# Sixteen block products for h, a tangent for the decay, and turned keys read in place

## The chip, the cores and the metric

The kernel runs on one core of a Trainium2 chip. The metric is the device time of one execution, in microseconds (us). A core has TensorE (PE in the profile; PEld are its weight loads), VectorE (DVE), ScalarE (ACT), GpSimd (POOL) and SyncE (SP), which issues the transfers. The engines run side by side and meet through semaphores; each takes its own instructions in a fixed order.

## The reference

A recurrent attention feeds a two-layer network. Per batch (4) and head (8), over 768 tokens, with head size 48:

```
f = 1 / (1 + exp(-f_logit))
for t in range(S):
    state = f[:, :, t, :, None] * state + outer(k[:, :, t], v[:, :, t])
    y[:, :, t] = q[:, :, t] @ state
x = y as (3072 tokens, 384)
h = x @ w_in                      # 384 x 2048
g = h * (1 / (1 + exp(-1.702 * h)))
out = g @ w_out                   # 2048 x 384
```

Everything is float32 on the chip. The weights come in as 64-bit floats and are turned into 32-bit ones on the way in.

## The kernel before

The 3072 tokens are 12 units of 256 tokens, three to a batch. `attention(n)` makes a list of parts for unit n: levels of scores (kinds V, V3, W), the turned keys (C, C2 or T), the state update (S), and the loading and turning of the next unit's decay, queries and keys (B, B2, K3). Each level multiplies queries by keys on PE (L392, tile `sc`), scales queries and keys by products of the decay on DVE (`promote`, L473 and L477), sets copies of them aside on ACT (L448 `Kc`, L454 `Qc`), and moves the scores under a mask into `A` (L421, L441). The products of the decay are `tot`, made by POOL in `begin_gates` (L383). At the end of a unit, y is copied from PSUM (L627, `yT`) and moved by transfers to `xT`, where the 384 features lie on the partitions (`to_x`).

The network's work is the fill between these parts. `merge(n, fill, ...)` emits the parts of unit n and, after each, as many matmul columns of the fill as the part's share says. For units 0 to 2 the network is done in blocks of four feature tiles (`mlp_blocks`), because the weights are still arriving and being converted by `convert` (L217 to L222). From unit 3 on, `mlp_unit(n)` does a whole unit: `mlp_h` (16 feature tiles of 128, three matmuls of 256 columns each, L785, with a gelu on ACT, L789), then `mlp_o7`, which makes the four blocks of the output with seven block products instead of eight (L762); its sums of g are made on DVE by `sums_of_a` and `last_sum` (L698 to L707), and its sums of w_out once by `sums_of_b`.

What sets the order: up to the merge of unit 3 every engine keeps the program's order; after that only PE does, and a scheduler orders the other engines. On PE, each network product waits in line; nothing overtakes it.

What the change touches:

- `turn` and `begin_f`: the decay is turned to features on partitions, by PE and ACT for units 0 to 2 (L344, L349), by DVE for later ones (L332), and goes through the sigmoid into `F` (L337 for later units, L355 for unit 2). Gelu and sigmoid are in different activation tables, so that ACT loads a table (an instruction ACT_TABLE_LOAD) at each change.
- `fetch_k`: keys of units 4 to 10 are turned by way of DRAM; two copies per unit (L555) put them in `kn` in the order in which the state update (L576) reads them.
- PSUM: four banks under one tag `mm`, taken in turn by whatever product comes next.
- `vr`, the values to be reversed, in two buffers; `g`, six quarter buffers.

Of the kernel before, what the change touches and what calls it, by code (L numbers as in the profile page):

```python
# [23 lines left out]
def kernel(  # L24
# [37 lines left out]
    P = 128  # L62
# [37 lines left out]
    A = const.tile([P, 2 * NP, 2, HS], F32, name="A")  # L100

    def keep_up(times, columns=384, of=None):

        if times:
            pt = ps.tile([P, columns], F32, tag="mm", name=f"idle_{next(serial)}", bufs=4)
        for _ in range(times):
            lhs, rhs = of or (ident, masks.rearrange("p l f t -> p (l f t)"))
            nc.tensor.matmul(pt, lhsT=lhs, rhs=rhs, start=True, stop=True)  # L108
# [117 lines left out]
    def convert():  # L226

        if state["begin"] < len(pairs) and len(todo) <= NOP // 2:
            begin_pair(state["begin"])
            state["begin"] += 1  # L230
        if todo and todo[0]:
            todo.pop(0)()
        if todo and todo[0] is None:
            todo.pop(0)
            state["done"] += 2
            fetch_weights()

# [40 lines left out]
    def load_v(n):  # L278


        if n >= NALL:
            return
        b, s0 = n // NU, n % NU * U
        vts[n] = ld.tile([P, 2, DM], F32, tag="vt", name=f"vt_{n}", bufs=2)
        vrs[n] = ld.tile([P, DM], F32, tag="vr", name=f"vr_{n}", bufs=2)
        nc.sync.dma_start(
            out=vts[n][:, 1].rearrange("p (h d) -> p h d", h=H), in_=v[b, :, s0:s0 + HALF, :].rearrange("h p d -> p h d")
        )
        for i in range(4):
            t0 = s0 + U - 32 * (i + 1)  # L290
            nc.sync.dma_start(
                out=vrs[n][32 * i:32 * (i + 1)].rearrange("p (h d) -> p h d", h=H),
                in_=v[b, :, t0:t0 + 32, :].rearrange("h p d -> p h d"),
            )
# [11 lines left out]
    def attention(n):  # L306
# [19 lines left out]
        def turn(j, outs, fn=None):  # L326

            if n >= N_FILL:
                for f in (1, 0):
                    out = outs(f)  # L330
                    at, step = (0, 1) if f else (HALF - 1, -1)
                    nc.vector.transpose(  # L332
                        view(out, at, [[HALF, NP], [step, R4], [R4 * step, 32]]),
                        by_half[:, j, f].rearrange("p a (j d) -> p (a j) d", j=R4)[:, :, :32],
                    )
                if fn:
                    nc.scalar.activation(F, F, fn)  # L337
                return
            for j0 in range(0, R, 4):
                pt = ps.tile([P, 4, P], F32, tag="mm", name=f"t_{n}_{j}_{j0}", bufs=4)  # L340
# [6 lines left out]
                for f in (1, 0):  # L347
# [4 lines left out]
                        fn if fn and n < N_FILL - 1 else AF.Copy,  # L352
                    )
            if fn and n == N_FILL - 1:
                nc.scalar.activation(F, F, fn)  # L355

        def begin_f():
            turn(0, lambda f: F[:, ORDER.index(f) * SLOT:(ORDER.index(f) + 1) * SLOT], AF.Sigmoid)
            if n >= N_FILL or (n == 1 and 0 == 0):
                load_raw(n + 1, 0)  # L360
# [164 lines left out]
        def turn_k(a0):  # L525
            if a0 == 0:
                new_kn()
            pt = ps.tile([P, 2, 2, P], F32, tag="mm", name=f"tkn_{n}_{a0}", bufs=4)
# [21 lines left out]
        def fetch_k(f):  # L550
            if f == 0:
                new_kn()
            z = mlp.tile([P, P, NP], F32, tag="sum", name=f"kt_{n}_{f}", bufs=3)
            nc.sync.dma_start(out=z.rearrange("p d a -> p (d a)"), in_=k_toks[n % 2][f].rearrange("t i x -> t (i x)"))
            nc.scalar.copy(t["kn"][:, :, f, :], z.rearrange("p d a -> p a d"))  # L555
# [12 lines left out]
        def _():  # L568
            add()
            pd = scores().rearrange("p h a s t -> p h (a s t)")  # L570
            for a in range(NP):
                for f in (1, 0):
                    for h in range(2):
                        for g in range(NG):
# [3 lines left out]
                                lhsT=t["kn"][g * HS:(g + 1) * HS, a, f, h * HS:(h + 1) * HS],  # L578
# [20 lines left out]
        def _():  # L599
# [21 lines left out]
            xT = xTs[n] = mlp.tile([P, NK, width(n)], F32, tag="xT", name=f"xT_{n}", bufs=3)  # L621
            for f in (1, 0):
# [6 lines left out]
            if n == NALL - 1:  # L629

                pl = ps.tile([P, NP], F32, tag="mm", name="y_last", bufs=4)
# [10 lines left out]
                to_x(lambda h: (yl[rows(h), :NK], lambda r, d: yl[r:r + d, NK]), xT[:, :, U:], 1)  # L642
# [48 lines left out]
    def sums_of_a(n, g, b):  # L691

        j = b % 2
        t0, t1 = slice(0, G), slice(G, 2 * G)
        tt = nc.vector.tensor_tensor
        if b < 2:
            g["S", j] = mlp.tile([P, FG, width(n)], F32, tag="g", name=f"S_{n}_{j}", bufs=6)
            tt(g["S", j][:, :, t1], g[j][:, :, t0], g[j][:, :, t1], ALU.subtract)  # L698
        else:
            tt(g[j][:, :, t1], g[j][:, :, t1], g[j + 2][:, :, t1], ALU.add)  # L700
            tt(g["S", j][:, :, t0], g[j][:, :, t1], g[j][:, :, t0], ALU.subtract)

    def last_sum(n, g):

        for j in range(2):
            by = slice(0, G)
            nc.vector.tensor_tensor(g[j + 2][:, :, by], g[j + 2][:, :, by], g["S", j][:, :, by], ALU.subtract)  # L707

    def mlp_o7(n, g):
        a = lambda i, j: lambda f: g[j * 2 + f // FG][:, f % FG, i * G:(i + 1) * G]  # L710
        s = lambda i: lambda f: g["S", f // FG][:, f % FG, i * G:(i + 1) * G]
        b = lambda i, j: lambda f: quarter(w_out, i, j)[:, f]
        T_ = lambda i: lambda f: T[i][:, f] if i < 4 else T[4](f)
        t = {}

        def out_(tt):
            if "o" not in g:
                g["o"] = mlp.tile([P, U // P, DM], F32, tag="osb", name=f"osb_{n}", bufs=1)
            return g["o"][:, tt]

        def row(name):
            t[name] = mlp.tile([P, HC], F32, tag=name, name=f"{name}_{n}", bufs=1)
            return t[name]

        def p1():
            nc.scalar.copy(row("p1"), t["X"])

        def p4():
            nc.scalar.copy(row("p4"), t["W"])

        def p2():
            nc.scalar.copy(out_(0)[:, :HC], t["X"])
            last_sum(n, g)

        def p6():
            nc.scalar.copy(row("p6"), t["Y"])

        def p5():
            nc.scalar.copy(row("p5"), t["Z"])

        def p7():
            nc.vector.tensor_tensor(row("u3"), t["p1"], t["Y"], ALU.add)
            nc.vector.tensor_tensor(out_(1)[:, :HC], t["u3"], t["p4"], ALU.subtract)
            nc.vector.tensor_tensor(out_(1)[:, HC:], t["u3"], t["p5"], ALU.add)
            store(n, 1, out_(1))

        def p3():
            nc.vector.tensor_tensor(out_(0)[:, HC:], t["p1"], t["Z"], ALU.add)
            nc.vector.tensor_tensor(out_(0)[:, HC:], out_(0)[:, HC:], t["p6"], ALU.add)
            store(n, 0, out_(0))  # L750


        products = (
            ("X", a(0, 0), b(0, 0), p1, True), ("W", a(1, 1), T_(4), p4, True), ("X", a(0, 1), b(1, 0), p2, False),
            ("Y", s(0), T_(2), p6, True), ("Z", a(1, 0), T_(1), p5, True), ("Y", s(1), T_(3), p7, False),
            ("Z", a(0, 1), b(1, 1), p3, False),
        )

        def one(bank, lhs, rhs, done, new, f):
            if new and f == 0:  # L760
                t[bank] = ps.tile([P, HC], F32, tag="mm", name=f"o_{n}_{bank}", bufs=4)
            nc.tensor.matmul(  # L762
                t[bank], lhsT=lhs(f), rhs=rhs(f), start=(new and f == 0), stop=(f == HF - 1), skip_group_check=True,
            )
            if f == HF - 1:
                done()
        return [(HC, lambda p=p, f=f: one(*p, f), 0) for p in products for f in range(HF)]


    xTs = {}  # L770

    def width(n):

        return U + (n == NALL - 1)

    def mlp_h(n, ffs, g, sums=False):
        t = {}

        def one(ff, c):
            if c == 0:  # L780
                if ff % FG == 0:
                    g[ff // FG] = mlp.tile([P, FG, width(n)], F32, tag="g", name=f"g_{n}_{ff}", bufs=6)
                t["ph"] = ps.tile([P, width(n)], F32, tag="mm", name=f"h_{n}_{ff}", bufs=4)
# [4 lines left out]
            if c == NK - 1:  # L788
                nc.scalar.activation(g[ff // FG][:, ff % FG, :], ph, AF.Gelu_apprx_sigmoid)  # L789
                if sums and ff % FG == FG - 1:  # L790
                    sums_of_a(n, g, ff // FG)
                if width(n) > U:

                    by = g[ff // FG][:, ff % FG, U:]
                    if ff == 0:
                        g["last"] = mlp.tile([P, 1, DM], F32, tag="sum", name="sum_last", bufs=3)
                        nc.vector.tensor_scalar(g["last"][:, 0], w_out[:, 0, :], by, None, op0=ALU.mult)
                    else:
                        nc.vector.scalar_tensor_tensor(
                            g["last"][:, 0], w_out[:, ff, :], by, g["last"][:, 0], op0=ALU.mult, op1=ALU.add  # L800
                        )
        return [(NK * U, lambda ff=ff: [one(ff, c) for c in range(NK)], ff // FG * NPC + ff % FG + 1) for ff in ffs]

    def mlp_o(n, ffs, g, done):
# [3 lines left out]
        def one(tt, ff):  # L808
            if ff == ffs[0]:
                t["po"] = ps.tile([P, DM], F32, tag="mm", name=f"o_{n}_{tt}_{ff}", bufs=4)  # L810
# [13 lines left out]
    def mlp_unit(n):  # L824
        g = {}

        def last_token():
            po = ps.tile([P, DM], F32, tag="mm", name="o_last", bufs=4)
# [4 lines left out]
        if width(n) > U:  # L833
            o.insert(3 * HF, (DM, last_token, 0))
        return mlp_h(n, range(NFF), g, True) + o
# [19 lines left out]
    def mlp_blocks(*blocks):  # L855

        hs, os = zip(*(mlp_block(n, r) for n, r in blocks))
        return sum(hs, []) + sum(os, [])
# [92 lines left out]
    UNIT = NFF * NK * U + U // P * NFF * DM  # L951

# [21 lines left out]
    fill += mlp_blocks((2, 0), (2, 1)) + mlp_blocks((2, 2), (0, 3)) + mlp_blocks((1, 3), (2, 3))  # L974
# [7 lines left out]
    for n in range(4, NALL):  # L982
        merge(n, fill, NFF * NK * U + 7 * HF * HC, late, chores=list(sums_of_b()) if n == 4 else ())
# [31 lines left out]
```

## Time and profile before

| | us |
|---|---|
| median of three runs | 628.49 |
| lowest, highest | 628.22, 629.21 |
| span of the profiled execution | 627.9 |
| PE, PEld busy | 602.8, 517.5 |
| DVE, ACT, POOL busy | 385.8, 260.3, 39.9 |
| h matmuls of all units (L785), busy | 257.4, of which 20.85 in the last unit |
| output matmuls of units 3 to 11 (L762), busy | 179.2 |

The profile is one execution. Busy time is the time in which an engine has at least one instruction running. A float32 matmul is two MATMUL records and two LDWEIGHTS records. "Idle before" names what an engine waited for last. The page's first parts give each engine's share, and then its busy tenths in forty slices of the span; the chain of work that ended last is followed back from the end, and its shares say which engine set the time.

### The profile page before, as it was taken

The numbers are of one execution on the slowest core, as the hardware profiler recorded it, in microseconds if no ns is written. First come the engines' busy times: TensorE is split into PE (matmuls) and PEld (weight loads), VectorE is DVE, ScalarE is ACT, GpSimd is POOL, SyncE is SP. The second block draws the span as 40 slices with busy tenths as digits, with TensorE's granted clock in tenths as the row PEclk, the third lists the DMA queues.
The fourth block names the chain that finished last, engine by engine and source line by source line (L and its number), as shares of the span: only waits on it lengthen the run. The fifth ranks groups of instructions, "written<-read, shape, count | busy, mean of one in ns | idle before, by whom it ended". The sixth has DMA issues, their size and how long they took to land.

```text
span 627.9 us, 17094 instructions
## 1 busy us (share of the span) xinstructions
PE 602.8 (96%) x7314; PEld 517.5 (82%) x7314; DVE 385.8 (61%) x632; ACT 260.3 (41%) x544; POOL 39.9 (6%) x91
## 2 busy tenths in 40 slices
PE   7958999889999999999999999999999999999997
PEld 5647776757678688989989989989989889889896
DVE  1778976575876755677566577656658645521441
ACT  3436543533244534543544454354354353233220
POOL 3010030020001001001001001001001001000000
PEclk9898999989999999999999999999999999999999
DMA  7646675652034444444452342552161121001000
GB/s 171 183 126 165 170 161 158 148 139 76 2 92 99 122 100 105 105 94 110 122 135 60 76 109 73 142 123 68 45 160 33 44 59 27 27 1 27 26 1 25
DMA packets 83308, 58.20 MB, mean 93 GB/s; under 512 B 33633, under 2 KB 75265, under 8 KB 83233
## 3 DMA queue, kind: packets, MB, share of 16 engines
q1 hardware_dynamic: 82192, 55.55, 35.4%
q10 hardware_dynamic: 1041, 1.57, 1.0%
q8 instruction: 57, 0.93, 0.7%
q14 instruction: 18, 0.15, 0.1%
HBM read 43.98 MB, written 8.39 MB: 83 GB/s over the span
## 4 chain that ended last, share of the span: by engine, by line
PE 87%; DVE 6%; ACT 3%; DMA 2%; issue 1%; SPq 1%; ACTq 0%; DVEq 0%
PE h L785 38%; PE o_X L762 8%; PE o_Y L762 8%; PE o L811 8%; PE o_Z L762 7%; PE sc L392 6%; PE o_W L762 4%; PE t L344 3%; PE y L616 2%; PE sc L576 2%; PE y L488 1%; PE idle L108 1%; DVE a L221 1%; DMA xT<-yT 1%; ACT yT L627 1%
## 5 line engine op out<-in xcount | busy, mean ns | idle before, releaser
L785 PE MATMUL h<-xT,w_in 128*128 128x256 f32 (+1 forms) x1152 | 257.4, 381 | 2.4 <-ACT g L789 1.9
L785 PEld LDWEIGHTS h<-xT,w_in 128*128 128x128 f32 x1152 | 216.4, 190 | 34.2 <-ACT g L789 2.1
L789 ACT ACTIVATE g<-h 128x256 f32<-128x256 f32 (+1 forms) x192 | 72.0, 383 | 156.8 <-PE h L785 156.5
L477 DVE TENSOR_TENSOR X<-X,tot 128x1024 f32<-128x1024 f32 x45 | 55.1, 1224 | 62.6 <-PE sc L392 49.4
L448 ACT COPY Kc<-X 128x512 f32<-128x512 f32 x72 | 48.0, 666 | 83.4 <-DVE X L477 51.3
L811 PE MATMUL o<-w_out,g 128*128 128x384 f32 x192 | 67.5, 501 | 3.0 <-DVE w_out L222 3.0
L811 PEld LDWEIGHTS o<-w_out,g 128*128 128x128 f32 x192 | 36.2, 194 | 26.0 <-DVE w_out L222 3.6
L762 PE MATMUL o_X<-w_out,g 128*128 128x192 f32 x288 | 52.6, 331 | 0.0
L762 PE MATMUL o_Y<-T,S 128*128 128x192 f32 x288 | 51.9, 329 | 0.0
L441 DVE COPY_PREDICATED A<-masks,sc 128x256 f32<-128x256 uint32 (+1 forms) x108 | 50.9, 534 | 0.1
L762 PEld LDWEIGHTS o_Y<-T,S 128*128 128x128 f32 x288 | 46.9, 190 | 1.5 <-issue 0.7
L762 PEld LDWEIGHTS o_X<-w_out,g 128*128 128x128 f32 x288 | 46.7, 190 | 1.0
L383 POOL TENSOR_TENSOR tot<-F 128x512 f32<-128x512 f32 x12 | 12.5, 1039 | 478.2 <-DVE st L594 429.3
L392 PE MATMUL sc<-X,Kc 48*64 48x64 f32 x1440 | 31.1, 224 | 10.7 <-ACT Kc L448 9.6
L392 PEld LDWEIGHTS sc<-X,Kc 48*64 48x64 f32 x1440 | 26.4, 138 | 18.0 <-ACT Kc L448 11.4
L332 DVE STREAM_TRANSPOSE X<-raw 128x512 f32<-128x512 f32 x36 | 37.9, 1101 | 2.9 <-PE y L616 2.8
L700 DVE TENSOR_TENSOR g<-g,g 128x512 f32<-128x512 f32 x18 | 12.5, 692 | 40.4 <-ACT g L789 40.4
L627 ACT COPY yT<-y 48x256 f32<-48x256 f32 x92 | 33.7, 366 | 7.8 <-PE y L616 5.3
L473 DVE TENSOR_TENSOR X<-X,tot 128x512 f32<-128x512 f32 x30 | 20.3, 688 | 13.1 <-PE sc L392 11.0
L383 POOL TENSOR_TENSOR tot<-tot 128x256 f32<-128x256 f32 (+4 forms) x60 | 24.6, 410 | 4.7
L762 PE MATMUL o_W<-T,g 128*128 128x192 f32 x144 | 24.9, 326 | 0.0
L762 PE MATMUL o_Z<-w_out,g 128*128 128x192 f32 x144 | 24.9, 326 | 0.0
(92 smaller groups left out, 629.1 us busy)
## 6 DMA issues: line engine op xcount, KB each, us to landing
bits<-in_moe_w_out_dram SPq DMA_DIRECT2D x8, 768.0 KB, 5.0
raw<-in_f_logit_dram SPq DMA_DIRECT2D x48, 96.0 KB, 2.3
raw<-in_k_dram SPq DMA_DIRECT2D x48, 96.0 KB, 2.3
raw<-in_q_dram SPq DMA_DIRECT2D x44, 96.0 KB, 2.3
bits<-in_moe_w_in_dram SPq DMA_DIRECT2D x7, 576.0 KB, 6.2
k_tok<-z SPq DMA_DIRECT2D x56, 64.0 KB, 1.8
kt<-k_tok SPq DMA_DIRECT2D x14, 256.0 KB, 2.8
out_dram<-osb SPq DMA_DIRECT2D x18, 192.0 KB, 1.8
```

The lines of the kernel that those rows point to most:

```text
L332: nc.vector.transpose(view(out, at, [[HALF, NP], [step, R4], [R4 * step, 32]]), by_half[:, j, f].rearrange("p a (j d) -> p (a j) d", j=R4) ...
L383: nc.gpsimd.tensor_tensor(tn, t2[:, :, 0], t2[:, :, 1], ALU.mult)
L392: nc.tensor.matmul(t["sc"][g * HS:(g + 1) * HS, h, a, s, :], lhsT=t["Kc", l][rows(h), x:x + HS], rhs=rhs(h, a, g), start=True, stop=True,)
L441: nc.vector.copy_predicated(out=view(A, at, dims), mask=mask.bitcast(U32), data=got)
L448: nc.scalar.copy(c.rearrange("p (n two m) -> p n two m", two=2, m=m), view(X, KF * SLOT, [[2 * m, SLOT // (2 * m)], [(KR - KF) * SLOT + m, ...
L473: nc.vector.tensor_tensor(x, x, y, ALU.mult)
L477: nc.vector.tensor_tensor(x, x, y, ALU.mult)
L627: copy(view(yT[rows(h)], at, [[U, NP], [step, HS]]), py[columns(h, g), g, :, f, :])
L762: nc.tensor.matmul(t[bank], lhsT=lhs(f), rhs=rhs(f), start=(new and f == 0), stop=(f == HF - 1), skip_group_check=True,)
L785: nc.tensor.matmul(ph, lhsT=w_in[:, c, ff * P:(ff + 1) * P], rhs=xTs[n][:, c, :], start=(c == 0), stop=(c == NK - 1))
L789: nc.scalar.activation(g[ff // FG][:, ff % FG, :], ph, AF.Gelu_apprx_sigmoid)
L811: nc.tensor.matmul(t["po"], lhsT=g[ff // FG][:, ff % FG, tt * P:(tt + 1) * P], rhs=w_out[:, ff, :], start=(ff == ffs[0]), stop=(ff == ffs[ ...
```

## The change

1. **h by sixteen products.** For units 3 to 11, w_in (15 of its 16 feature tiles) is seen as 3 by 3 blocks: three groups of five feature tiles by three groups of 128 input features. x of a unit is 3 by 2 blocks: three groups of features by two halves of 128 tokens. The plain product of such blocks takes 18 block products; a bilinear scheme does it in 16, of sums of blocks. `mlp_h16` runs them in four lanes, each with a PSUM bank of its own. A lane is a chain of products that add up in the bank; on the way the running sum is read out after some products (by an ACT copy the first time a block of h is met, by a DVE add the second time), so that one bank serves several blocks. The sixteenth feature tile is done as before (`left`).
2. **Sums of w, once.** `sums_of_w` makes the blocks' sums in unit 3 (seven new tiles N1 to N7) and some in place of blocks of w_in that earlier units no longer need (`middle`, `last`), 14 operations on POOL and 4 on DVE.
3. **Sums of x, per unit.** `sums_of_x` makes eleven operations of 128x128 on POOL once xT is there.
4. **Decay by the tangent.** sigmoid(x) = 0.5 tanh(x/2) + 0.5. ACT makes the tanh, POOL the 0.5 and 0.5. Where the kernel before has twenty table loads, the built kernel has two.
5. **Turned keys read with a step.** The copies to `kn` go; the state update reads the weights from the fetched tile with a step of four elements.
6. **Room.** PSUM banks are named (`mm0` to `mm3`, function `bank`), a few products move to the scores' buffer `sc`, `vr` has one buffer, `g` three half buffers. `mlp_o7` keeps its sums in the output tile instead of rows of its own, and takes the feature tiles in the order in which h gets ready. `sums_of_a` runs after all of h instead of between its quarters.

```diff
-                    nc.scalar.activation(F, F, fn)
+                    fn()
...
+        def half_up():
+            nc.gpsimd.tensor_scalar(F, F, 0.5, 0.5, op0=ALU.mult, op1=ALU.add)
+
+        def sigmoid():
+            nc.scalar.activation(F, F, AF.Tanh, scale=0.5)
+            half_up()
...
         def fetch_k(f):
-            if f == 0:
-                new_kn()
-            z = mlp.tile([P, P, NP], F32, tag="sum", name=f"kt_{n}_{f}", bufs=3)
+            z = t["kt", f] = mlp.tile([P, P, NP], F32, tag="sum", name=f"kt_{n}_{f}", bufs=3)
             nc.sync.dma_start(out=z.rearrange("p d a -> p (d a)"), in_=k_toks[n % 2][f].rearrange("t i x -> t (i x)"))
-            nc.scalar.copy(t["kn"][:, :, f, :], z.rearrange("p d a -> p a d"))
+        def turned_k(p, a, f, d):
+            return t["kt", f][p, d, a] if n in CARRY else t["kn"][p, a, f, d]
...
+    CHAINS = (
+        (("D5", "b21", 3), ("N6", "E12", 2), ("C4", "E4", 4), ("N3", "E15", 0), ("a00", "E6", 1), ("N4", "E10", 5)),
+        (("N5", "b21", None), ("N1", "b11", 1), ("D11", "E11", None), ("D8", "E3", 0)),
+        (("a22", "E3", None), ("D9", "E9", 4), ("N7", "b10", None), ("N2", "E14", 2)),
+        (("a10", "E0", None), ("D2", "b11", 3)),
+    )
+    LANES = ((0, 0), (1, 3)), ((0, 1), (1, 1)), ((0, 2), (1, 2)), ((0, 3), (1, 0))
...
+            for t in range(nt):
+                x = (ts.start + t) * P
+                nc.tensor.matmul(
+                    ph[:, t], lhsT=WA[a][:, x:x + P], rhs=E[n][b], start=(i == 0 and t == 0),
+                    stop=(i == len(CHAINS[chain]) - 1), skip_group_check=True,
+                )
+            if out is None:
+                return
+            to = where(group, out // 2, out % 2)
+            scale = -1.0 if out in NEGATIVE else 1.0
+            if out == CHAINS[0][-1][2]:
+                nc.scalar.activation(to, ph, AF.Gelu_apprx_sigmoid, scale=scale)
+            elif (group, out) not in begun:
+                begun.add((group, out))
+                nc.scalar.copy(to, ph)
+            else:
+                nc.vector.tensor_tensor(to, to, ph, ALU.add)
+                nc.scalar.activation(to, to, AF.Gelu_apprx_sigmoid, scale=scale)
...
-        return mlp_h(n, range(NFF), g, True) + o
+        return mlp_h16(n, g) + o
...
-        merge(n, fill, NFF * NK * U + 7 * HF * HC, late, chores=list(sums_of_b()) if n == 4 else ())
+        merge(n, fill, H16 + 7 * HF * HC, late, chores=list(sums_of_b()) if n == 4 else ())
```

A chain's entry is the block or sum of w, the block or sum of x, and the block of h that is read out after it. A pair in LANES is a group (0: three feature tiles of each block, 1: two) and a chain; PE takes one product of each lane in turn.

## The prediction

> **What bounds the kernel now.** I read the page first: busy shares, slices, shares of the chain.
>
> ```profile
> PE 602.8 (96%) x7314; PEld 517.5 (82%) x7314; DVE 385.8 (61%) x632; ACT 260.3 (41%) x544; POOL 39.9 (6%) x91
> PE   7958999889999999999999999999999999999997
> PE 87%; DVE 6%; ACT 3%; DMA 2%; issue 1%; SPq 1%; ACTq 0%; DVEq 0%
> ```
>
> TensorE is the bound, and after the first quarter nothing interrupts it. The chain in order of time shows this stage by stage (start, length, both us):
>
> ```profile
> 451.47 18.33 PE h L785 x84
> 471.76 2.80 PE o_X L762 x16
> 497.35 18.33 PE h L785 x84
> ...
> 584.31 20.85 PE h L785 x96
> ```
>
> A steady unit lasts 497.35 - 451.47 = 45.9 us. Its h is 96 records (48 matmuls, two records each): 20.85 us when nothing lies between, as in the last unit. One steady unit by engine:
>
> ```profile
> core 0: us, PE busy (x) PEld busy (x) DVE busy (x) ACT busy (x) POOL busy (x), PEclk, DMA share, GB/s
> 310.20:355.90 45.70, 45.70 (x593) 41.95 (x592) 27.68 (x46) 21.05 (x43) 2.81 (x6) 1.00 0.41 98
> ```
>
> PE has no gap at full clock; DVE has 18 us free, ACT 25, POOL 43. So a steady unit gets shorter by what PE is spared, and longer only by what PE is made to wait.
>
> The edit gives PE fewer columns but more weight loads, so I need the shortest distance of two matmuls with 128 moving columns and a full 128-column f32 weight. No row shows that pair. The nearest are two small forms, in which the load is long for the streaming (first PE in order of time, then the weight loads by shape, mean ns after the comma):
>
> ```profile
> 333.17 1.10 PE L576 MATMUL sc<-vt,kn 64*64 64x48 f32 x64
> 566.08 0.48 PE L634 MATMUL y_last<-q_end,st 48*48 48x1 f32 x16
> ```
>
> ```profile
> L785 PEld LDWEIGHTS h<-xT,w_in 128*128 128x128 f32 x1152 | 216.4, 190 | 34.2 <-ACT g L789 2.1 <-issue 1.3 <-DVE sum L850 0.2
> L576 PEld LDWEIGHTS sc<-vt,kn 64*64 64x64 f32 x768 | 12.5, 135 | 1.0 <-ACT kn L555 0.6 <-issue 0.4
> L634 PEld LDWEIGHTS y_last<-q_end,st 48*48 48x48 f32 x16 | 0.5, 122 | 0.0
> ```
>
> L576 runs four tiles side by side, so 64 records are 16 rounds; less the last record's own 0.22 us, (1.10 - 0.22)/15 = 59 ns a round, for 64 weight columns and 48 moving ones. L634 runs two side by side: (0.48 - 0.18)/7 = 43 ns for 48 weight columns and one moving. Streaming can't be the limit there: h streams 256 columns in 20.85/96 = 217 ns, 0.84 ns a column, which is 40 ns for 48. The load is, and it counts 135 - 59 = 76 or 122 - 43 = 79 ns less than its record. For 128 columns: 190 - 77 = 113 ns.
>
> Last, where PE does wait, and ACT around one such wait:
>
> ```profile
> PE sc L392 <- ACT Kc L448: 9.6, 3, 6.7
> PE o L811 <- DVE w_out L222: 3.0, 1, 3.0
> ...
> PE h L785 <- ACT g L789: 1.9, 1, 1.9
> ```
>
> ```profile
> 115.53 1.28 ACT L337 ACT_TABLE_LOAD   x1
> 116.82 1.06 ACT L337 ACTIVATE F<-F 128x1024 f32<-128x1024 f32 x1
> 117.78 0.89 ACT L217 ACTIVATE a<-bits 128x768 f32<-128x768 f32 x1
> 118.69 1.28 ACT L789 ACT_TABLE_LOAD   x1
> 119.99 0.38 ACT L789 ACTIVATE g<-h 128x256 f32<-128x256 f32 x1
> ```
>
> The 1.9 us wait of h at 118.6 us ends with the last of these lines: two table loads, 2.57 us, stand ahead of the gelu that frees a bank.
>
> [...] Streaming here takes two records of about 109 ns. [...]
>
> **The change part by part.**
>
> *h by sixteen products.* Per unit 16 products of 5 tiles are 80 matmuls with 128 moving columns, 160 records; the sixteenth tile keeps 3 matmuls of 256 columns, 6 records. At 113 ns: 160 x 0.113 + 6 x 0.217 = 19.4 us for 20.85: 1.45 us less. Ends: 109 ns if only streaming counts (2.1 us less), [...] The two small forms give 111 to 114; I take 112, which is 19.2 us a unit: 1.6 us less, times nine units (3 to 11) = 14.4 us.
>
> *Evacuation.* A unit loses 16 gelus (383 ns) and gets 10 copies out of PSUM, 10 DVE adds and 13 gelus. By L848 and L850 a copy of 384 elements takes 476 ns, an add 548; those of 256 about 0.38 and 0.43. DVE: 10 x 0.49 = +4.9 us, to 32.6 of 44. ACT: +9.9 - 6.1, less two table loads (2.6) and two kn copies (L555, 1.13 us each, 2.3): 20.0 us. Both have room; the danger is when. Each of four lanes has one bank, and its next product overwrites or adds to what was just read. It comes back after three other products: 3 x 3 x 0.224 = 2.0 us in the group of three tiles, 1.34 in that of two. Out of that go about 0.2 us from the end of streaming to the start of ACT (as in the h rows) and 0.4 to 0.55 for the read: 0.6 to 1.2 us for standing in a queue. DVE's queue there holds transposes (1.10 us) and one promotion (1.22), and the order of the built kernel puts one or two of these ahead of an add, with the six S sums after all of them. Walking that order with these durations, most adds end 0.3 us or more before PE needs them and one or two per unit come close. I take 0.3 us per unit, 2.7 us; ends 0 and 1.5 us per unit.
>
> *Sums of x.* Eleven POOL operations of 128x128; the tot row of that shape takes about 0.40 us: 4.4 us. Hidden: the last xT transfer is issued about 7 us before h starts (o products between), and the first two products need no E. 0 us; high end 1 us per unit.
>
> *Sums of w.* 14 POOL operations of 128x640 and 4 on DVE. A tot of 128x512 takes 1.04 us, so about 1.3 us each. The order has most of them in unit 3 where POOL waits anyway (429 us in all), but unit 3's own sums of x stand behind the last three. 0.5 us, ends 0 and 3.
>
> *Tanh.* 20 table loads become 2. In steady units they cost nothing, as PE never waits for ACT there; the wait at 118.6 us goes: -1.9 us. POOL gets one 128x1024 pass per unit [...], ahead of tot, with idle time before it. 0.
>
> *Turned keys with a step.* The kn copies were off the path. The 16 rounds of L576 now read weights 16 bytes apart. Low end 0; [...] I take 0.5.
>
> *Others* (banks by name, vr single, output sums: one DVE add fewer behind the last product) -0.3 us.
>
> Sum: 628.5 - 14.4 + 2.7 + 0.5 - 1.9 + 0.5 - 0.3 = 615.6.
>
> **Rivals.**
> - *Loads don't hide*: [...] For: [...] no full-size pair is in the trace. Against: the two small forms, [...]
> - *Lanes wait*: 1.5 us per unit eat the gain: 628.5 - 14.4 - 1.9 + 13.5 + 1 = 627, little or no change. For: DVE at 74% with 1.1 us pieces in a strict order, ACT copies behind gelus that wait for DVE. Against: the free time above, and the last unit has nothing else in the queues.
> - *Everything hides*: 109 ns, no waits, no price for the step: 628.5 - 2.1 x 9 - 1.9 - 0.3 = 607.
>
> **How the numbers follow.** Forecast 0.58; lanes wait 0.19 (a third of it on the slow side); everything hides 0.15; loads don't hide 0.08. Predicted is the forecast, 615.6. The range of 608 to 628 holds the forecast with its ends, nearly all of the third rival and most of the second; the first is left out. Faster 0.58 + 0.15 + 0.10 = 0.83; same 0.03; slower 0.08 + 0.06 = 0.14.
>
> **What would show it.** h records of 128 columns 112 ns apart, and the last unit's h at about 19.2 us for 20.85; a steady unit of 44.3 to 44.7 us for 45.9; PE's waits for ACT and DVE at the h lines under 0.5 us per unit; two table loads and no gap near 118 us; rounds of the turned keys at 59 ns. The prediction is wrong if h records stand 130 ns or more apart, or if PE's idle time ahead of the h lines passes 10 us in all.

## The result, and the profile after

The changed kernel takes 637.7 us (636.3 to 637.9) beside 628.9 (628.2 to 629.3) for the kernel before, here with a fourth run: a ratio of 1.0137, 95% interval 1.0118 to 1.0155. It is slower by 8.9 us, where 13 us less was forecast and 628 was the upper end of the range.

The page of the changed kernel: busy shares, PE's busy tenths in forty slices, and the chain's shares by engine.

```profile
PE 602.2 (95%) x7944; PEld 535.8 (84%) x7944; DVE 437.8 (69%) x717; ACT 252.9 (40%) x565; POOL 138.4 (22%) x216
PE   7869999989959999999999999999999999999997
PE 79%; DVE 12%; ACT 4%; issue 3%; DMA 1%; ACTq 0%; SPq 0%; DVEq 0%
```

TensorE is busy for as long as before although h has become shorter, and VectorE now has 12% of the chain for 6%. The slices have a 5 in the twelfth place, 175 to 191 us, which the kernel before doesn't have. Then the chain in order of time, for a steady unit and for the last one.

```profile
319.77 1.34 PE h L904 x12
...
322.20 8.70 PE h L904 x76
...
337.40 2.94 PE h L904 x24
340.35 1.30 PE h_left L924 x6
...
342.69 1.90 PE sc L595 x64
...
366.45 1.34 PE h L904 x12
...
594.60 17.86 PE h L904 x160
612.46 1.31 PE h_left L924 x6
```

The same view of the kernel before has, for the state update of a steady unit:

```profile
287.26 0.92 PE sc L576 x64
```

Three things stand in them. The last unit's h takes 17.86 + 1.31 = 19.17 us for 20.85: the products themselves did what was forecast (19.2). The state update (`sc`, L595) takes 1.90 us, for 0.92 before with the same 64 records. And a steady unit from h to h is 366.45 - 319.77 = 46.7 us, not 44.5, and h was held up on the way: the chain leaves it after 76 records and comes back for the last 24.

What the changed kernel gains and loses against the one before. Units are counted from 0 as in the code; "the third unit" is unit 3, the first whose h takes sixteen products, and "the fourth" is unit 4.

| part | read from | us |
|---|---|---|
| h | last unit, 19.17 for 20.85 us, times nine: -15.1; new starts of h after other work, 1.8 us in all for 0.9: +0.9 | -14.2 |
| tanh | first h to third unit's h, the kernel before with this part alone: 163.9 for 165.6 | -1.7 |
| stepped keys | steady unit of the kernel before with this part alone: 46.81 for 45.84, seven units | +6.8 |
| sums of w | first h to third unit's h: 174.3, and 163.7 without the sums | +10.6 |
| waits inside h | spacing of the records over 112 ns: 8.8 us in nine units, less the 1.8 of the new starts | +7.0 |
| sum | | +8.5 |

The medians differ by 8.9 and the spans of the two profiled executions by 8.2, so about half a microsecond is left over. The stretch "first h to third unit's h" leaves out the start, which moves by up to 3 us from one execution to another.

**The stepped keys.** The view of the state update's line in the changed kernel (shortest, median, longest ns): `kt` is the tile read with a step of four elements, `kn` the one without, still used by the other units.

```profile
L595 PEld LDWEIGHTS sc<-vt,kt x448: 188/213/215, 249.3 to 529.2; 64*64 64x64 f32 x150
L595 PEld LDWEIGHTS sc<-vt,kn x320: 129/135/135, 32.5 to 569.5; 64*64 64x64 f32 x160
```

A weight load of the same size is 78 ns longer, and the group of sixteen rounds per unit is 1.90 - 0.92 = 0.98 us longer, 61 ns a round.

**The third unit's sums.** The waits of TensorE between 100 and 240 us (total, times, longest), and two windows of 5 us (busy us of PE, PEld, DVE, ACT, POOL, then the granted clock, the share of its full clock that TensorE was given):

```profile
PE h L975 <- ACT kn L552: 7.0, 1, 7.0
PE h L975 <- DVE sum L1028: 1.5, 1, 1.5
```

```profile
180.00:185.00 5.00, 0.00 (x0) 0.00 (x0) 5.00 (x6) 1.12 (x2) 0.59 (x1) 0.72 0.17 40
185.00:190.00 5.00, 4.54 (x13) 3.73 (x14) 4.96 (x4) 1.84 (x5) 4.98 (x3) 0.60 0.78 193
```

TensorE stands still for 7 us, and then has 0.60 of its clock on average: eight of h's records there start some 427 ns apart instead of 216. That second price, some 1.7 us here (8 x 0.21), was not in the forecast. The other wait, 1.5 us for an output sum of VectorE's, lies 5 us ahead; 7.0 + 1.7 + 1.5 = 10.2 of the 10.6 us. The trace has half rate (a granted clock of 0.50) from 182.2 us, 3.7 after TensorE stopped, to 189.0, 3.5 after it went on. A shorter stop, of 1.87 us, brought it too, as "The stepped read alone" shows below.

Who holds TensorE up? The timeline of the changed kernel there, start and length in us:

```profile
179.12 2.28 DVE L702 TENSOR_TENSOR T<-T,w_out 128x768 f32<-128x768 f32 x1
...
181.79 1.99 DVE L340 STREAM_TRANSPOSE F<-raw 128x512 f32<-128x512 f32 x2
...
183.88 1.06 ACT L370 ACTIVATE F<-F 128x1024 f32<-128x1024 f32 x1 [8.43 <-DVE F L340]
184.84 1.05 ACT L552 COPY kn<-tkn 128x512 f32<-128x512 f32 x2
185.02 1.05 POOL L367 TENSOR_SCALAR F<-F 128x1024 f32<-128x1024 f32 x1 [4.43 <-ACT F L370]
...
185.46 4.59 PE L975 MATMUL h<-xT,w_in 128*128 128x256 f32 x12 [6.97 <-ACT kn L552]
```

Read it from the bottom. TensorE waits for a bank that holds turned keys; ScalarE's copy of them stands behind the tanh of the next F; the tanh waits 8.43 us for VectorE to turn F; and VectorE turns F late because what stands ahead of it has become slow. GpSimd's own queue holds nobody up: GpSimd is idle for 4.43 us before it scales this F. The groups of VectorE's operations from 150 to 200 us, count, busy us and mean ns after the bar; first the changed kernel, then the one before:

```profile
L228 DVE TENSOR_TENSOR w_out<-a,s 128x768 f32<-128x768 f32 x2 | 4.0, 2005 | 0.0
L702 DVE TENSOR_TENSOR T<-w_out,T 128x768 f32<-128x768 f32 x2 | 3.2, 1620 | 0.0
```

```profile
L222 DVE TENSOR_TENSOR w_out<-a,s 128x768 f32<-128x768 f32 x2 | 1.9, 954 | 0.0
L679 DVE TENSOR_TENSOR T<-w_out,T 128x768 f32<-128x768 f32 x2 | 1.9, 950 | 0.0
```

The same operations take 1.7 to 2.1 times as long on average while GpSimd makes its sums of w, and GpSimd's sums take 1.55 to 2.42 us where 1.3 was assumed. The operations shown have two inputs. VectorE's one-input step of the conversion (L225, L226) slows too, from 0.55 to as much as 1.89 us, while its addition of a 128x384 bank (L1028) stays at 0.54. Through what the two engines slow each other is not shown.

**The lanes.** The timeline of the changed kernel inside h of the steady unit above:

```profile
334.02 0.85 ACT L464 COPY Kc<-X 128x512 f32<-128x512 f32 x1 [0.56 <-DVE X L340]
...
334.78 0.37 ACT L916 COPY g<-h 128x256 f32<-128x256 f32 x1
...
335.20 0.71 PE L904 MATMUL h<-E,N 128*128 128x128 f32 x4 [0.31 <-ACT g L916]
...
335.79 1.23 DVE L493 TENSOR_TENSOR X<-X,F 128x1024 f32<-128x1024 f32 x1 [1.35 <-ACT Qc L470]
...
336.94 0.41 DVE L918 TENSOR_TENSOR g<-g,h 128x256 f32<-128x256 f32 x1
...
337.40 0.52 PEld L904 LDWEIGHTS h<-xT,N 128*128 128x128 f32 x4 [0.29 <-DVE g L918]
```

A bank's copy waits behind a set-aside of the keys, which itself waited 0.56 us for VectorE's turn of X; an addition waits behind a promotion. The spacing of h's records shows three such waits here, 0.47, 0.40 and 0.26 us, with about 0.1 us more at each new start: 1.3 to 1.5 us per unit in units 3 to 8.

### The profile page after: what moved, and what is told of

It is laid out like the page before. It is cut to its first block, busy times and chain, and to the rows that moved or that the text cites. A ratio compares the mean times of both kernels' runs of the same rounds, so it can differ in the third digit from the quotient of the medians.

```text
span 636.1 us, 18686 instructions
## 1 busy us (share of the span) xinstructions
PE 602.2 (95%) x7944; PEld 535.8 (84%) x7944; DVE 437.8 (69%) x717; ACT 252.9 (40%) x565; POOL 138.4 (22%) x216
## 4 chain that ended last, share of the span: by engine, by line
PE 79%; DVE 12%; ACT 4%; issue 3%; DMA 1%; ACTq 0%; SPq 0%; DVEq 0%
PE h L904 21%; PE o_Y L787 12%; PE h L975 8%; PE o L989 7%; PE o_Z L787 7%; PE sc L408 6%; PE o_X L787 4%; PE o_W L787 4%; PE sc L595 3%; PE h_left L924 2%; PE y L635 2%; PE t L352 2%; PE y L504 2%; ACT Kc L464 2%; DVE X L493 1%
## 5 line engine op out<-in xcount | busy, mean ns | idle before, releaser
L904 PE MATMUL h<-E,w_in 128*128 128x128 f32 (+1 forms) x630 | 87.4, 278 | 1.1 <-ACT g L913 0.7
L904 PEld LDWEIGHTS h<-E,w_in 128*128 128x128 f32 x630 | 77.8, 192 | 3.2 <-ACT g L913 1.3
L975 PE MATMUL h<-xT,w_in 128*128 128x256 f32 x288 | 69.0, 392 | 9.0 <-ACT kn L552 7.0
L918 DVE TENSOR_TENSOR g<-g,h 128x384 f32<-128x384 f32 (+3 forms) x90 | 43.0, 488 | 41.3 <-PE h L904 39.9
L975 PEld LDWEIGHTS h<-xT,w_in 128*128 128x128 f32 x288 | 54.6, 195 | 19.4 <-ACT kn L552 7.4
L916 ACT COPY g<-h 128x256 f32<-128x256 f32 (+3 forms) x90 | 37.6, 426 | 55.4 <-PE h L904 55.1
L919 ACT ACTIVATE g<-g 128x384 f32<-128x384 f32 (+3 forms) x90 | 41.4, 470 | 33.9 <-DVE g L918 33.4
L904 PE MATMUL h<-E,N 128*128 128x128 f32 (+1 forms) x360 | 50.0, 277 | 1.5 <-ACT g L916 0.8
L904 PEld LDWEIGHTS h<-E,N 128*128 128x128 f32 x360 | 44.6, 192 | 2.8 <-ACT g L916 1.4
L408 PE MATMUL sc<-X,Kc 48*64 48x64 f32 x1440 | 31.3, 224 | 10.6 <-ACT Kc L464 6.7
L904 PE MATMUL h<-xT,N 128*128 128x128 f32 (+1 forms) x270 | 39.3, 276 | 0.3
```

The costliest lines, as they stand in the source:

```text
L408: nc.tensor.matmul(t["sc"][g * HS:(g + 1) * HS, h, a, s, :], lhsT=t["Kc", l][rows(h), x:x + HS], rhs=rhs(h, a, g), start=True, stop=True,)
L904: nc.tensor.matmul(ph[:, t], lhsT=WA[a][:, x:x + P], rhs=E[n][b], start=(i == 0 and t == 0), stop=(i == len(CHAINS[chain]) - 1), skip_grou ...
L916: nc.scalar.copy(to, ph)
L918: nc.vector.tensor_tensor(to, to, ph, ALU.add)
L919: nc.scalar.activation(to, to, AF.Gelu_apprx_sigmoid, scale=scale)
L975: nc.tensor.matmul(ph, lhsT=w_in[:, c, ff * P:(ff + 1) * P], rhs=xTs[n][:, c, :], start=(c == 0), stop=(c == NK - 1))
```

## The experiments

The theory after the result: three terms were mis-sized, the stepped keys, the sums of w and the lanes' waits, each by a mechanism of its own. The rivals to it: that the keys' layout acts through ScalarE's copies and not through the weight loads; that VectorE's own four sums of w cost the time, and not its slowing beside GpSimd's; that the lanes wait for one engine's queue. Each run has its own comparison with the kernel before, which took 628.9 to 629.5 us in these.

**Keys without a step.** The tile is laid out so that a weight's columns are neighbours, and fetched in four transfers; no copy. The tile into which VectorE turns the keys on their way to DRAM is laid out alike (not shown).

```diff
-            z = t["kt", f] = mlp.tile([P, P, NP], F32, tag="sum", ...)
-            nc.sync.dma_start(out=z.rearrange("p d a -> p (d a)"), in_=k_toks[n % 2][f].rearrange(...))
+            z = t["kt", f] = mlp.tile([P, NP, P], F32, tag="sum", ...)
+            for a in range(NP):
+                nc.sync.dma_start(out=z[:, a].rearrange("p (i d) -> p i d", d=32), in_=k_toks[n % 2][f][:, :, a * 32:(a + 1) * 32])
...
-            return t["kt", f][p, d, a] if n in CARRY else t["kn"][p, a, f, d]
+            return t["kt", f][p, a, d] if n in CARRY else t["kn"][p, a, f, d]
```

> The changed kernel with the turned keys laid out in DRAM and in the fetched tile so that the 64 weights of a matmul lie one after the other; no copy on ACT, four fetches for one. Theory (the step of 16 bytes slows each weight load of the state update): the 64 records of the state update take 0.96 us for 1.90 in units 4 to 10, 7 x 0.93 = 6.5 us less, so 631.2 us for 637.7. Rival (PE would wait for something else in that place): the group gets shorter and the time stays at 636 to 638.

It took 627.9 us (626.1 to 631.3), ratio 0.9981 (0.9968 to 0.9994): 9.8 us less than the changed kernel, and 3.3 less than expected. The state update is back at its old length. Timelines of the changed kernel and of this one (1.10 was its length in the kernel before, in the same view):

```profile
249.38 2.08 PE L595 MATMUL sc<-vt,kt 64*64 64x48 f32 x64
```

```profile
248.03 1.10 PE L598 MATMUL sc<-vt,kt 64*64 64x48 f32 x64
```

That is some 6.8 of the 9.8 us. Of the other 3, 2.3 are shorter waits in h, 6.5 us in all for 8.8. The edit does more here than undo the step: VectorE's turn of the keys, which now writes neighbours, takes 0.70 us for 1.13, fourteen times, and the order of ScalarE's and VectorE's work inside h is another. Which of these shortens the waits was not taken apart.

**Keys copied, as before the change.**

```diff
+            nc.scalar.copy(t["kn"][:, :, f, :], z.rearrange("p d a -> p a d"))
...
-            return t["kt", f][p, d, a] if n in CARRY else t["kn"][p, a, f, d]
+            return t["kn"][p, a, f, d]
```

> The changed kernel with the two copies per unit of the kernel before put back (ACT, 1.13 us each), so that the weights are read without a step. If the step alone costs and ACT has room: 631 us, as with the other layout. If the lanes wait because of ACT's queue: the two copies stand ahead of lane copies and give back 0.5 to 1 us per unit, 634 to 638 us, with more PE idle at the h products.

634.1 us (633.7 to 635.3), ratio 1.0076 (1.0047 to 1.0106). The step is gone and only 3.6 us come back: the waits inside h grow to 1.56 to 1.66 us per unit in units 3 to 9. By name 5.2 of 5.9 us are for ScalarE's reads of a bank (3.6 for copies, 1.6 for gelus that read one), and the copies of the keys stand ahead of such reads. In the lanes the copies give back about half of what the unstepped read saves; the kernel before had no lanes to delay, and there the copies were free.

**The stepped read alone, in the kernel before.** The same edit of the read as in the change, nothing else.

> The kernel before, with the turned keys read with a step as the only edit: no copy by ScalarE, weights four elements apart. If the step costs what the groups of 64 records show (0.93 us more per unit in seven units) and TensorE has nothing to hide it, 635 to 636 us with 628.9 before. If the ScalarE copy had been on the path, or the loads hide beside other work, 628 to 631.

637.4 us (634.9 to 637.5), ratio 1.0101 (1.0075 to 1.0128), so 8 us slower by the medians. Its steady unit is 46.81 us for 45.84: 0.97 in each of seven units, 6.8 us. The group's 0.98 us shows in full: nothing in TensorE's queue hides it. Another 1.7 us falls between 112 and 148 us, and it is the clock. Both kernels have the same stop of 1.87 us at 118.5 us; the windows 0.9 us after it, first of this run, then of the kernel before (granted clock third from the end):

```profile
121.30:124.60 3.30, 3.30 (x10) 2.59 (x9) 0.69 (x2) 0.68 (x2) 0.00 (x0) 0.50 0.95 196
```

```profile
121.30:124.60 3.30, 3.30 (x20) 2.63 (x22) 0.71 (x2) 1.08 (x3) 0.00 (x0) 1.00 0.86 173
```

These 3.3 us at half rate cost 1.65. So a stop of the same length cost this in one execution and not in the other, and what decides it is not shown. The five runs fall in two groups, 637.4 to 637.5 and 634.9 to 635.3, the second with the higher mean clock (0.989 and 0.992 for 0.987); it is the one that fits the expected 635 to 636.

**Tanh alone, in the kernel before.** The three edits of the decay (`AF.Tanh` with scale 0.5, and `half_up` on GpSimd).

> The kernel before, with the decay by tanh and GpSimd's scaling as the only edit. The prediction gave this part 1.9 us, all of it the table's load at 118 us: 627.0 with 628.9 before. The changed kernel's TensorE stood 1.65 us ahead at 156 us, which would give 627.2. If GpSimd's scaling of F lies on a path of its own, no gain or a loss: 628.5 to 631.

627.3 us (626.7 to 628.9), ratio 0.9965 (0.9947 to 0.9982). The wait at 118 us is gone, the steady unit is unchanged at 45.83, and the stretch to the third unit's h is 1.7 us shorter. The term held.

**No sums of w.** The sums are left out; the products read a plain block of w_in in their place.

```diff
-            WA[f"N{i}"] = const.tile([P, ROW * P], F32, name=f"N{i}")
-        by = lambda op: lambda out, x, y: nc.gpsimd.tensor_tensor(WA[out], WA[x], WA[y], op)
+            WA[f"N{i}"] = WA["a00"]
+        by = lambda op: lambda out, x, y: None
...
         def both_minus(out, x, y):
+            return
```

> The changed kernel without any of the 18 sums of w (14 on POOL, 4 on DVE); the products read plain blocks of w_in in their place, so the output is not the reference's. Theory (the sums in unit 3 delay DVE, DVE delays ACT, ACT delays PE): the 7.0 us wait of h for ACT goes and unit 3's h starts 9 to 11 us earlier, 627 to 629 us. Rival (the wait comes from the tanh and its place in ACT's queue): the wait stays, 636 us or more.

**Only VectorE's four sums of w.** The edit of `by` alone: GpSimd's fourteen are left out, and N4 and N7, which VectorE makes, keep their tiles.

> The changed kernel with the 4 sums of w on DVE kept and the 14 on POOL left out (plain blocks in their place, so the output is not the reference's). If POOL slows DVE while both run: DVE's operations of unit 3 are back at their times of before (0.95 us for a sum of w_out for 2.2) and the time is within 3 us of the run without any sums, 628 to 631 us. If DVE's own four sums are the delay: 634 to 637 us.

626.5 us (625.2 to 627.6; ratio 0.9951, 0.9936 to 0.9967) and 626.8 (625.2 to 629.7; ratio 0.9961, 0.9947 to 0.9974). In both, the 7 us wait is gone and the way from the first h to the third unit's h is 163.7 us, as with tanh alone (163.9). So VectorE's own four sums are hidden, and GpSimd's fourteen make the whole 10.6 us; a sum of T on VectorE is back at 0.95 us. Both times lie 0.5 to 1.2 us under what was expected.

**Sums of w spread.** From here on with unstepped keys. The sums wait in a list, and one is issued behind every fourth piece of network work.

```diff
-        by = lambda op: lambda out, x, y: nc.gpsimd.tensor_tensor(WA[out], WA[x], WA[y], op)
+        by = lambda op: lambda out, x, y: pending.append(lambda: nc.gpsimd.tensor_tensor(WA[out], WA[x], WA[y], op))
...
                     emit()
                     done += w
+                    if pending and next(items_done) % 4 == 0:
+                        pending.pop(0)()
```

> The changed kernel with the keys fetched so that a weight is read without a step (627.9 us by itself), and with the eighteen sums of w handed out one by one, each behind four further blocks of MLP work, so that GpSimd's scaling of the fourth unit's F stands behind four of the sums and no longer behind eight. If it is GpSimd's sums at 160 to 190 us, in a heap ahead of that scaling and against VectorE, that make the first half late, some 4 to 9 us come back: 619 to 624 us, h of the third unit starts by 220 us, and TensorE's wait of 7 us for ScalarE's copies goes below 3. If it is the sums' total, wherever they lie, 627 to 629 us.

624.8 us (623.9 to 625.0), ratio 0.9913 (0.9891 to 0.9934). The wait for the key copies goes from 7.0 to 3.0 us, the clock still drops (0.93 from 150 to 200 us), and the stretch is 170.2 us for 174.1 with unstepped keys alone. That is a little less than was expected (624 at most, and h of the third unit by 220 us, where it starts at 222.2).

**Sums of w late.** None before the place where GpSimd scales the fourth unit's F, so that VectorE turns that F undisturbed; then one behind every second piece.

```diff
         def half_up():
+            if n == N_FILL + 1:
+                state["go"] = True
...
-                    if pending and next(items_done) % 4 == 0:
+                    if pending and "go" in state and next(items_done) % 2 == 0:
```

> Unstepped keys, and the sums of w handed out only from the place where GpSimd scales the fourth unit's F, one behind every two blocks, so that none of them runs while VectorE turns that F. If it is this delay of tanh, and of the key copies behind it, that cost TensorE 7 us of wait and a clock of 0.60 after it, the wait goes wholly (3.0 were left when the sums were spread, at 624.8 us), h of the third unit starts at 216 to 218 us, and the kernel takes 617 to 620. If the sums only move the same delay into the third unit's own turns and promotions, 624 to 628.

619.8 us (618.7 to 621.3), ratio 0.9846 (0.9822 to 0.9870). The window that stood still, in this kernel:

```profile
180.00:185.00 5.00, 5.00 (x18) 3.09 (x17) 5.00 (x5) 0.38 (x1) 2.57 (x3) 1.00 0.57 143
```

TensorE is busy throughout at full clock. VectorE is just as full in this window as before, and that no longer matters: what TensorE was waiting for is already done. The stretch is 167.2 us: 7 of the 10.6 us are back. The third unit's h starts at 219.0 us, 1 later than expected; this execution took 621.3 us, 1.4 over the median, at a mean granted clock of 0.986, where the other five have 0.989 to 0.992.

**All sums of w on VectorE.** Spread as above.

```diff
-        by = ... pending.append(lambda: nc.gpsimd.tensor_tensor(WA[out], WA[x], WA[y], op))
+        by = ... pending.append(lambda: nc.vector.tensor_tensor(WA[out], WA[x], WA[y], op))
```

> Unstepped keys, the sums of w spread one behind every four blocks, and all eighteen on VectorE, none on GpSimd. If GpSimd and VectorE hold each other up in these sums, VectorE does them in about 0.8 us each, its other operations keep their times of the kernel before (0.95 us for a sum of T), and the kernel gains over the spread sums' 624.8: 617 to 621 us. If VectorE's own time is what is short there, the eighteen sums' 14 us lie in its queue ahead of F's turns, and it is 625 to 630.

621.0 us (619.7 to 621.6), ratio 0.9867 (0.9845 to 0.9888). The wait for the key copies is 0.5 us and the stretch 167.0. VectorE makes a sum of w in 0.81 to 1.06 us and a sum of T in 0.95. The fourteen that it takes over are 4.5 + 4.1 + 3.2 + 0.8 = 12.6 us of work. In the changed kernel the slowed operations beside GpSimd's fourteen are 13.2 us longer in all than their lines' medians elsewhere. So GpSimd's sums cost VectorE about as much time as making them itself.

**Set-asides on GpSimd.** Unstepped keys, sums as in the change. The copies ahead of a bank's copy (`Kc`, `Qc` of the first level, units after the third) go to GpSimd.

```diff
-            nc.scalar.copy(
+            copy = nc.gpsimd.tensor_copy if n > N_FILL and l == 0 else nc.scalar.copy
+            copy(
```

> The same kernel with unstepped keys (627.9 us by itself), and with the first two set-aside copies of each unit after the third moved from ScalarE to GpSimd, since they stand in ScalarE's queue ahead of the copies that empty h's banks. If ScalarE's queue makes the lanes wait, TensorE's waits at the lines of h go from about 0.9 us per unit to under 0.4, and the kernel gains 3 to 5 us: 623 to 625. If VectorE's additions, or the order of the lanes, make them wait, or if GpSimd's copies slow VectorE by as much, nothing is gained: 627 to 630.

629.1 us (626.8 to 630.8), ratio 0.9986 (0.9972 to 0.9999), where unstepped keys alone gave 627.9. The waits stay at 0.6 to 1.1 us per unit, and by name half of them are now for VectorE's additions. Taking these copies out of ScalarE's queue is no remedy by itself.

**Promotions in halves.** Unstepped keys, spread sums.

```diff
-                nc.vector.tensor_tensor(x, x, y, ALU.mult)
+                for i in range(2):
+                    nc.vector.tensor_tensor(x[:, i], x[:, i], y[:, i], ALU.mult)
```

> The kernel with unstepped keys and spread sums (624.8 us), with each promotion of keys and queries on VectorE (1.2 us for 128x1024) made in two halves, so that additions that empty h's banks wait for half as much. If the lanes wait for what stands ahead of VectorE's additions, TensorE's waits at h's lines go from 0.85 to 1.2 us per unit to about 0.5, and it is 621 to 623 us. If they wait for the way from TensorE over VectorE to ScalarE as a whole, or the scheduler puts nothing between the halves, 624 to 626.

626.9 us (625.7 to 629.6), ratio 0.9966 (0.9953 to 0.9980): 2 us more than without the split, 0.85 to 1.2 us of waits per unit as before. The edit also reached the third unit (3.7 us of new waits for set-asides), so it is no clean test of VectorE's queue; it shows only that this is no remedy.

**Lanes mixed.** Counting h's records shows where the waits lie. Of 160, the first 48 pass in rounds of 12 matmuls (four lanes, one for each of three feature tiles; the expectation says "blocks", and each is two records), the last 68 in rounds of 8 or 9, as by then most lanes have come to their groups of two. All waits of over 0.12 us in units 3 to 8 of the changed kernel lie at records 110 to 136, in these short rounds, where a bank comes back after 6 or 7 matmuls, 1.3 to 1.6 us. In this run two lanes start with their groups of two, so that each round is 10 matmuls. Base: unstepped keys and late sums.

```diff
-    LANES = ((0, 0), (1, 3)), ((0, 1), (1, 1)), ((0, 2), (1, 2)), ((0, 3), (1, 0))
+    LANES = ((0, 0), (1, 3)), ((1, 1), (0, 1)), ((0, 2), (1, 2)), ((1, 0), (0, 3))
```

> The kernel with unstepped keys and late sums of w (619.8 us), with the lanes of h mixed: two of the four lanes start with their chain of two-block groups, so that every round of lanes is 10 blocks, where now the first rounds are 12 and the last 8. If TensorE waits because in the short rounds a bank must be read out within 6 blocks (1.34 us at 112 ns a record), the waits go from 0.8 to 1.3 us per unit to 0.3 or less: 615 to 617.5 us. If the queues of ScalarE and VectorE are behind by themselves, whatever the lanes' order, the waits stay near 0.9 and the time at 619 to 621.

617.5 us (617.1 to 618.7), ratio 0.9812 (0.9791 to 0.9833). The waits fall from 6.6 to 4.0 us over all units, of which 1.8 are common to all; in one steady unit h runs through:

```profile
399.08 16.28 PE h L913 x144
```

In most others a wait of 0.3 to 0.5 us is left. So the order of the lanes makes about half of it, and the time is at the upper edge of what was expected.

**Without the additions.** Base as in the last run, lanes as in the change; gelu takes the second read alone.

```diff
-                nc.vector.tensor_tensor(to, to, ph, ALU.add)
-                nc.scalar.activation(to, to, AF.Gelu_apprx_sigmoid, scale=scale)
+                nc.scalar.activation(to, ph, AF.Gelu_apprx_sigmoid, scale=scale)
```

> The kernel with unstepped keys and late sums of w (619.8 us), without VectorE's additions of the second half of h's sums: gelu is taken of the second half alone, straight from the bank by ScalarE, so a part of the computation is left out. If VectorE's additions and what stands ahead of them hold the banks, the waits go to 0.3 us per unit or less, 615 to 617. If it is ScalarE's queue, which now does one thing more from the bank, they stay at 0.8 to 1.3 or grow: 619 to 623.

613.6 us (613.3 to 615.4), ratio 0.9752 (0.9729 to 0.9774), 6.2 less than its base. The waits inside h are down to 0.1 to 0.3 us per unit, 1.8 in all, which are the new starts, and the steady unit is 44.3 to 44.5 us, the length that the prediction gave. ScalarE reads all banks here, behind the same set-asides, and isn't late. So the lanes wait only with VectorE's additions there. By which way is not told apart, as the edit takes them all: an addition is late behind VectorE's other work; a gelu waits in ScalarE's order for an addition, with bank copies behind it; or a set-aside waits for VectorE's turn of X, which stands behind additions.

**Mixed lanes with the sums on VectorE, late.** The edits of "All sums of w on VectorE" and "Lanes mixed" together, with the sums late.

> Unstepped keys, the sums of w late and all on VectorE, and the mixed lanes. The sums on VectorE stood 1 us behind the late ones on GpSimd by their medians, and 0.7 ahead by the span. With the lanes' waits gone 615 to 618; 619 to 622 if the order of the lanes is not what makes them.

622.1 us (621.7 to 622.7), ratio 0.9881 (0.9861 to 0.9902), a miss. Waits inside h are as in the mixed run (3.9 us), but TensorE waits 3.2 us for VectorE's masked moves ahead of the third unit: eighteen sums fall where VectorE is needed. In these runs sums on VectorE did better early (621.0 without mixed lanes), sums on GpSimd late (619.8 for 624.8).

The best kernel here is the one with unstepped keys, late sums on GpSimd and mixed lanes: 617.5 us, 1.9% faster than the kernel before and 3.2% faster than the changed one (617.5 / 637.7).

## Why the prediction was wrong

The forecast's sum was 615.6, the change gives 637.7, and nearly all of the 22 us lies in three of its terms. One of its signs of being wrong came: PE's idle time ahead of the h lines was to stay under 10 us, and is 11.3.

- *h by sixteen products* held. Records of 128 columns stand 111 to 112 ns apart, as the two small forms had said, and the last unit's h takes 19.17 us for a forecast of 19.2. So the rival "Loads don't hide" is refuted, though the kernel did get slower; its price for loads that don't hide was the author's estimate, which no trace showed.
- *Tanh* held: -1.7 for -1.9, two table loads of 1.28 us for twenty.
- *Turned keys with a step* failed. The prediction took 0.5 us from a low end of 0. Measured are 0.98 us per unit by the group, 0.97 by the edit alone, 6.8 us in all, and gone when it is undone. Its own trace gives a high end, an estimate: rounds of 59 ns, if they doubled, would cost 16 x 0.059 x 7 = 6.6 us. It had what it needed to take that end: it had just found that in these rounds the load (59 ns a round) and not the streaming (40 ns) is the limit, so anything longer in the load had to show. By how much a step makes a load longer, no trace showed before the result.
- *Sums of w* failed: "0.5 us, ends 0 and 3", measured 10.6. It counted GpSimd's idle time and looked for who waits for GpSimd. Nobody waits for a sum of w in the trace. The cost went through VectorE, whose two-input operations slowed from 0.95 to as much as 2.3 us at the place where it was fullest (35.6 of 50 us busy before, 44.5 after), then through F's turn, tanh and the key copies in ScalarE's order to TensorE, which stood for 7 us and then had 0.60 of its clock from 185 to 190 us. The order of the built kernel has nine of GpSimd's sums ahead of its scaling of the fourth unit's F; what was missing was a price for two engines at once.
- *Evacuation* failed in size: 0.3 us per unit taken, end 1.5, measured 1.1 to 1.3 in units 3 to 8 (after the common 0.2), 7.0 us in all for 2.7. The mechanism was right and named, with the 1.34 us in which a bank comes back, and so was the rival "Lanes wait". Walking the order with single durations shows where an add is close, not what VectorE's and ScalarE's queues do to each other when each waits for the other. Without the additions the waits are gone; which of the two queues' waits weighs most stays open.
- *Sums of x* held as far as it was seen: no wait of TensorE for them is in the trace. One takes 0.46 us in the median, at most 1.52; the row of `tot` of that shape is 0.48 us, not 0.40.

In the forecast's terms: 615.6 + 6.3 (keys) + 10.1 (sums of w) + 4.3 (lanes) + 0.2 (h) + 0.2 (tanh) = 636.7, against 637.7. With the three mended as far as was found, 617.5.

## What to carry to other kernels

On an engine that never waits, price each change of what it reads as time of its own: where the weight load was the limit here, a step in it made each round 119 ns for 58. Before moving work to an idle engine, ask which busy engine slows while it works (VectorE's 128x768 additions here, 0.95 us to as much as 2.3) and what stands in that engine's queue behind the slowed operations; idle time of the helper says nothing. And where banks are read out by engines that also wait for each other, the shortest round sets the slack, so make the rounds even (waits in h of 4.0 us for 6.6 here).

## What was not expected of the hardware

- A 64x64 float32 weight load with its columns 16 bytes apart takes 213 ns for 135, and a round of four such tiles 1.90 / 16 = 0.119 us for 0.92 / 16 = 0.058.
- VectorE's 128x768 additions take 0.95 us, and 1.8 to 2.3 when GpSimd adds 128x640 tiles beside them (one, as the first such sum began, stayed at 0.95); GpSimd's take 1.55 to 2.42 us, where VectorE makes such a sum in 0.81 at best.
- VectorE's turn of a 128x512 tile takes 1.13 us when it writes 16 bytes apart, and 0.70 when it writes neighbours.
- The clock after a stop of TensorE doesn't go by its length alone. In the changed kernel a stop of 7.0 us was followed by half rate from 182.2 to 189.0 us, with h records 427 ns apart instead of 216, and one of 2.94 us near 127 us by half rate from 131.0 to 134.4. One of 1.87 us at 118.5 us was followed by half rate with the stepped read alone (0.50, ten records in 3.3 us), and by none in the kernel before (1.00, twenty).
